# The taps of the short convolution in units 1 to 4 as 64x64 quarters of the array, on two token halves

## The chip, the cores and the metric

The kernel runs on one core of a Trainium2 chip. That core has a matrix engine (TensorE, PE in the profile, with its weight loads as PEld), a vector engine (VectorE, DVE), a scalar engine (ScalarE, ACT), GpSimd (POOL) and a queue engine (SyncE, SP) that issues almost every transfer of this kernel; the transfers themselves run on 16 DMA engines. The metric is the device time of one execution in microseconds (us). The median of three runs counts.

## The reference, cut to what matters

The reference is a block with two branches for 2048 tokens (S) and 640 channels (D). The part around the change is the first branch, a short causal convolution of `k` over four tokens, a product with `v`, and a long convolution over all tokens by a Fourier transform:

```python
for t in range(ks):                       # ks = 4 taps, one weight per channel and tap
    k_shift = k_shift + k_pad[:, t:t + S, :] * shift_k[:, ks - 1 - t][None, None, :]
kv = k_shift * v
...
kv_f = rfft(kv_pad); kf_f = rfft(ssm_k_pad)     # per channel, over 2*S tokens
y = irfft(kv_f * kf_f)[:S] + kv * ssm_D
x = x + ga * (h * y)                            # h: layer norm of x, modulated
```

The second branch is a gated MLP with a 2048x2048 mix over tokens. It uses all channels of the new `x` and so starts when the first branch is through. All inputs are bf16.

## The kernel before, in words

**Units.** The first branch is cut by channels into five units of 128 (0 to 4). For each unit `load_kv` brings `k` and `v` from device memory into a tile of the kind `big` with a transposing transfer, so that channels lie on the 128 partitions and tokens in a row (L520). Two such tiles exist, so unit 2 takes the place of unit 0. Unit 0 loads `k` and `v` in two halves of 1024 tokens each, the others in one transfer of 2048 tokens each.

**Taps.** `short_conv` makes four diagonal 128x128 matrices `dg` from the unit's tap weights (L531 to L539) and lets TensorE multiply `k`, shifted by 0 to 3 tokens, by them, so that four matmuls add up to one chunk of 512 tokens in PSUM (tile `sm`, L543 to L547). VectorE multiplies the chunk by `v` (L549 to L552). A unit has four chunks. The result is written to a scratch tensor in device memory, `kv_scr` (L558), and read back from there as `X<-kv_scr` in the layout of the Fourier transform (L389). After that a unit has two stages of matmuls forward (`s<-F1bd,X`, then `pu<-X,M`), a product with the transformed filter, and the same backward (`pz`). The filter itself comes in as `X<-in_A_ssm_k_dram` and goes through the same forward stages.

**The order.** Every step is recorded as an operation with its readers and writers, and a table of numbers, `ORDER`, says in which order all operations are issued. Each engine takes its own operations strictly in that order. On SP this means one queue for all loads and stores: the tapped products' store, the read-back, the filter's loads, the rows of `x` (`xt<-in_A_q_dram`), the modulation weights (`wm`) and the `k` and `v` of later units stand one behind the other. PE has one queue as well: the taps of a unit stand between transform matmuls of earlier units, so a tap that waits for its `k` holds back everything behind it. The names that matter below: `big` (k and v of a unit), `dg` (tap matrices), `sm` (PSUM of the taps), `X` (input of the transform), `kv_scr` (scratch), `ZT<-Z` (a transposing transfer inside the core for the end of a unit), `bsp` (a column of biases of the second branch, loaded later on by L1065).

Of the kernel before, what the change touches and what calls it, by code (L numbers as in the profile page):

```python
# [40 lines left out]
S2 G101 D18 S524 A1 D0 D100 G5 P7 A4 A10 D102 S82 G103 D121 D122 D104 D115 A531 S19 D13 D14 S20 D6 S21 A16 P1033 D532  # L41
A105 A106 S523 D15 A23 P1032 P8 P1035 S83 D11 P26 P24 S22 A533 D17 D116 D86 P1034 G107 G109 P145 A124 A146 P148 G108
D25 D110 A118 A117 A111 A112 A123 G36 D27 A149 A147 S88 D127 P28 D150 D113 P30 D87 D31 P154 A114 D527 D125 G119 P151
A155 A156 D29 A152 G126 D153 P133 D528 A128 A534 D134 G48 P139 D120 P159 P161 A160 D90 A140 S32 P136 P157 P142 A162
D529 P227 D137 P171 S34 A158 D530 A143 P163 D535 P39 A228 S33 A172 S35 P41 S84 G536 D138 A164 P167 S85 A168 P233 S46
P173 D42 A175 D40 S47 P176 A174 D177 A178 P43 D537 D44 P179 G553 P182 P37 D181 D549 D38 P165 G72 A180 A184 S45 A183
D141 G135 S526 P185 D186 A234 P229 G187 A166 P195 P211 G188 P49 P189 D196 P169 A230 D212 P231 A170 D50 P201 S3 D202
P217 P53 D218 A232 G144 A190 G550 P203 A542 P191 S89 S525 G197 G551 A204 P9 A12 P205 G198 G213 D54 P55 A543 P251 D192
P51 P247 D56 G130 G131 A252 G214 D206 P253 D52 A248 P239 A254 S565 A240 D538 P221 P199 D222 P257 G554 P241 P566 S91
A544 A200 D258 P568 P255 D539 P249 D256 P215 G223 D216 A242 G60 A545 A250 P193 G555 D93 P291 G224 S57 D292 S570 P225  # L50
S58 A540 P237 A238 P301 G207 P269 A194 P235 S59 P219 A569 A567 P571 D541 A302 G208 D270 A236 G271 P573 D546 A226 D220
D574 P307 P209 P245 G547 A552 P259 D572 D272 P67 D260 A308 P305 A246 P243 D548 D591 D561 D129 P265 A210 D68 G562 D261
A306 A244 A557 P61 P285 D62 A563 G262 P303 P65 P263 S92 P63 A304 D286 P325 A564 D266 S94 A326 D66 P295 P273 D296 P275
P327 A264 D276 S575 G707 A274 D676 S70 P267 D64 D297 P321 A328 A322 G556 G558 D651 D649 P309 A310 G670 P329 D96 P315
A330 S71 P576 P313 P331 P293 D559 D298 D577 A316 D597 S69 G287 P323 A314 D560 D595 S599 A332 P333 D598 D653 A324 G612
D593 P77 G288 P375 P349 A268 P277 D334 A294 A376 D78 D350 G594 S95 P343 P377 A132 D344 G596 P578 P319 G709 A378 P299
A278 P317 P73 D592 P379 D614 A320 A318 G335 A300 P311 P365 P289 D579 A380 G336 S97 G345 D616 A312 G652 P381 P337 D74
D654 P600 D674 D346 P279 D366 D601 D280 A290 G615 P369 P602 D370 P79 P347 G281 A382 A338 G282 D603 D80 A348 P387 P399
G371 A388 P359 P604 G372 G710 D605 P353 P283 G618 A400 D360 P401 P606 A284 D354 G355 D99 P351 P339 D340 A402 P403 D711
D607 A404 P383 D613 D619 P75 P385 A384 P405 P373 S580 A386 P395 D352 G361 G356 A406 G650 S620 A396 P397 P449 D362 A374  # L60
A398 P407 D76 P367 P413 A450 G617 P363 S81 D408 A368 D414 P391 P453 D364 P621 D622 P389 A392 A454 P439 P357 G655 G677
A390 P623 P451 A452 P427 D440 A358 D624 P341 G409 D428 P625 P417 G410 G611 G429 P455 D626 P411 P627 G430 S98 P443 P581
A342 A456 D418 P471 A412 P473 D444 P431 A472 A474 P393 P423 D628 G419 D656 A394 A582 G420 P475 P441 P465 A476 P479 D424
D432 G672 D442 P433 S657 A466 P421 A480 P461 G609 G629 D434 P477 A422 D639 P425 P658 G445 P467 A462 G446 A478 D671 P517
D659 A468 P447 A426 G435 P660 G436 D518 P457 A458 P437 A448 D661 P481 P463 G608 D482 P662 D663 G675 D631 G519 G520 G483
G484 A438 A464 P415 S583 P507 A416 P664 P497 D508 P584 D498 P485 P459 A486 P521 G634 S678 A460 A522 P491 G509 P1037
P501 D510 D633 A585 D492 P511 P487 D502 A512 G708 P499 A500 G493 G494 G503 P469 S586 G673 P495 D488 G504 S756 D665 P513
A470 P489 D514 P679 A496 G667 D680 P515 G712 D630 G666 A490 D632 P681 P505 A516 D682 P683 D637 D684 A506 P715 P719 A720
D716 P685 D686 P721 D687 A722 P717 P587 P723 D718 P725 D688 P726 P724 D689 D727 D728 D729 D730 D758 D759 D731 G669 P735
G692 D736 A588 P742 G760 D732 D761 G762 P1036 A763 G713 D690 P749 D734 P764 D743 D733 D691 D771 D766 S757 P765 D772  # L70
# [12 lines left out]
D1001 P1018 A949 P985 D998 D1062 G960 A947 D1002 D899 D1008 P989 A1019 A986 P956 D961 P1024 P1012 A964 D963 D962 D1009  # L83
A990 D987 A965 D991 P1014 D995 D984 A957 D988 A1025 A1013 G1026 A1015 D1051 P944 D1066 P1070 D1027 A945 D1063 A1030
P1020 A1029 S1042 D1064 P1072 A1071 D1028 A1021 D1031 D1065 P1074 D1068 D1067 P1077 D1075 P1081 P1022 A1073 P1076 D1069
D1078 D1082 D1079 P1083 S1080 P1010 P1016 A1017 D1084 A1011 S1085 D1047 A1023 D1061 D1046 D1048 D1060
"""


# [1215 lines left out]
```

## Time and profile before

| | |
|---|---|
| median of 3 runs | 312.03 us (311.89 to 312.06) |
| span of the profiled execution, first to last instruction | 309.7 us |
| outside the span (median less span) | 2.3 us |
| PE busy | 295.1 us (95%) in 2485 matmuls |
| DVE, POOL, ACT busy | 272.4, 186.2, 164.1 us |
| DMA, mean over the span | 146 GB/s, 45.23 MB in 127954 packets |

The profiled execution's own time is its span and the 2.3 us around it, taken from the median, since the profile gives only the span. The page has the busy time of each engine, the span in 40 slices, the chain of work that ended last, and the costliest groups of instructions. A group names the line, the engine, the operation and `out<-in` by the program's names. A line of a helper (L244 is the helper that issues a matmul) stands for all its callers, so such groups are told apart by their tiles. `SPq` is the issue of a transfer by SP; the time of such a row is the time the issue took, not the transfer's. How long a transfer takes to land stands in the list of DMA issues.

### The profile page before, as it was taken

To read this page: it belongs to the slowest core of one execution; us is meant where nothing else is said; L and a number is where in the kernel's file an instruction comes from. 1 tells how busy PE (TensorE), PEld (TensorE's weight loads), DVE (VectorE), ACT (ScalarE), POOL (GpSimd) and SP (SyncE) were. 2 spreads that over 40 slices of the span, in tenths; PEclk is the share of its full clock that TensorE was granted. 3 is DMA by queue.
4 is the path that set the end of the run, shared out by engine and by line. 5 is a ranking of instruction groups with operands and counts; after the bars stand their busy time and mean duration, and the time that the engine had idled before them with its cause. 6 is when DMAs were issued, how large, how long until landed. Compare 5 with 4: busy or idle time off the path is not lost.

```text
span 309.7 us, 6534 instructions
## 1 busy us (share of the span) xinstructions
PE 295.1 (95%) x2485; PEld 195.4 (63%) x2485; DVE 272.4 (88%) x532; ACT 164.1 (53%) x298; POOL 186.2 (60%) x209
## 2 busy tenths in 40 slices
PE   6979999999999999899999999998899999999995
PEld 1357678797889998755554555555455656565554
DVE  7797999999999999998859788999999878888574
ACT  4799699989787864466647799031111111021110
POOL 5724955856869999695705312049658474573922
PEclk9799999999999999999999999999999999999999
DMA  7999999999674949505898800073387593730323
GB/s 176 224 251 200 243 299 199 249 254 207 170 158 115 184 110 273 211 3 108 191 181 180 150 1 1 2 145 51 73 167 150 132 194 73 168 80 21 83 55 110
DMA packets 127954, 45.23 MB, mean 146 GB/s; under 512 B 117071, under 2 KB 127156, under 8 KB 127924
## 3 DMA queue, kind: packets, MB, share of 16 engines
q1 hardware_dynamic: 127770, 44.78, 65.5%
q8 instruction: 19, 0.31, 0.4%
q14 instruction: 11, 0.09, 0.1%
q10 hardware_dynamic: 154, 0.05, 0.1%
HBM read 16.11 MB, written 5.24 MB: 69 GB/s over the span
## 4 chain that ended last, share of the span: by engine, by line
PE 40%; DVE 6%; DMA 4%; SPq 4%; POOL 2%; issue 1%; ACT 0%; DVEq 0%; ACTq 0%
PE ps L1012 20%; PE po L1178 7%; PE pu L244 4%; PE pz L244 4%; DMA Z<-Z 3%; SPq L973 2%; PE pz L1012 2%; PE pu L1012 1%; DVE S L987 1%; PE po L1139 1%; SPq L1073 1%; DMA uT<-u 1%; POOL Z L844 1%; DVE V L1160 1%; POOL xt L697 1%
## 5 line engine op out<-in xcount | busy, mean ns | idle before, releaser
L244 PEld LDWEIGHTS <-Z 128*128 128x128 bf16 x320 | 31.1, 98 | 28.4 <-issue 1.2
L244 PE MATMUL pu<-X,M 128*128 128x128 bf16 (+1 forms) x480 | 45.9, 237 | 0.4 <-DVE Tf L461 0.3
L244 PEld LDWEIGHTS <-M 128*128 128x128 bf16 x480 | 37.1, 98 | 5.3 <-issue 0.6
L475 POOL TENSOR_TENSOR W<-Tf 128x256 bf16<-128x256 f32 x43 | 31.3, 745 | 12.7 <-DVE Tf L461 5.0
L1012 PEld LDWEIGHTS <-S 128*128 128x128 bf16 x256 | 25.0, 98 | 21.2
L244 PE MATMUL pu<-big,Z 128*128 128x432 bf16 x160 | 33.6, 346 | 0.5 <-ACT M L919 0.4
L244 PE MATMUL pz<-big,Z 128*128 128x432 bf16 x160 | 32.6, 346 | 0.1
L1196 ACT COPY O<-po 128x320 f32<-128x320 f32 x7 | 3.0, 427 | 55.9 <-PE po L1178 55.9
L247 ACT CAST X<-s 128x1024 bf16<-128x1024 f32 x30 | 30.7, 1024 | 3.5 <-PE s L244 3.4
L461 DVE TENSOR_TENSOR Tf<-pu,KH 128x1024 f32<-128x1024 f32 x25 | 30.0, 1214 | 1.4 <-PE pu L244 1.0
L1012 PEld LDWEIGHTS <-wT 128*128 128x128 bf16 x192 | 18.7, 98 | 17.6 <-issue 2.0
L244 PEld LDWEIGHTS <-G 128*128 128x128 bf16 x330 | 25.0, 98 | 3.3 <-issue 0.6
L247 ACT CAST KH<-pu 128x512 bf16<-128x512 f32 x40 | 23.5, 598 | 6.0 <-PE pu L244 6.0
L247 ACT CAST Z<-pz 128x512 bf16<-128x512 f32 x34 | 19.9, 599 | 8.2 <-PE pz L244 8.1
L1199 POOL TENSOR_TENSOR O<-O,xt 128x320 f32<-128x320 f32 x7 | 6.3, 906 | 28.0 <-ACT O L1198 28.0
L1012 PE MATMUL ps<-T,S 128*128 128x432 bf16 x112 | 22.7, 346 | 0.0
L1012 PE MATMUL ps<-X,wT 128*128 128x432 bf16 x112 | 22.7, 346 | 0.0
L244 PE MATMUL sm<-big,dg 128*128 128x512 bf16 (+1 forms) x80 | 21.3, 395 | 0.7 <-ACT dg L535 0.7
L1012 PE MATMUL ps<-X,S 128*128 128x432 bf16 x112 | 21.6, 346 | 0.0
L244 PEld LDWEIGHTS <-X 128*128 128x128 bf16 x288 | 18.2, 97 | 5.2 <-issue 1.4
L244 PE MATMUL s<-F1bd,X 128*128 128x256 bf16 x128 | 19.2, 273 | 0.3 <-ACT X L247 0.3
L925 DVE BATCH_NORM_STATS2 stz<-X 128x6 f32<-128x432 bf16 x32 | 17.8, 589 | 1.6 <-ACT X L919 1.6
(208 smaller groups left out, 679.9 us busy)
## 6 DMA issues: line engine op xcount, KB each, us to landing
wm<-in_w_mod_dram SPq DMA_DIRECT2D x6, 800.0 KB, 6.1
xt<-in_A_q_dram SPq DMA_DIRECT2D x4, 640.0 KB, 5.2
out_dram<-ot SPq DMA_DIRECT2D x15, 160.0 KB, 2.2
big<-in_B_w_in_dram SPq DMA_DIRECT2D x2, 1080.0 KB, 10.7
X<-in_A_ssm_k_dram SPq DMA_DIRECT2D x4, 512.0 KB, 7.0
kv_scr<-big SPq DMA_DIRECT2D x4, 512.0 KB, 3.2
X<-kv_scr SPq DMA_DIRECT2D x4, 512.0 KB, 4.5
w_o<-in_B_w_out_dram SPq DMA_DIRECT2D x6, 160.0 KB, 3.4
```

What stands on the lines that cost most here:

```text
L244: nc.tensor.matmul(o, lhsT=w, rhs=x, start=start, stop=stop)
L247: (e.copy if e is nc.scalar else e.tensor_copy)(dst, src)
L461: e.tensor_tensor(T_[:], (tl[pu] if src is None else tl[src])[:, :, :, None, :].to_broadcast(shape), tl[KH][:, :, None, :, :].to_broadcast ...
L475: e.tensor_tensor(tl[W][:, :, o, :], T_[:, :, 0, o, :], T_[:, :, 1, 1 - o, :], op=ALU.add if o else ALU.subtract)
L697: op("GD" if u < NU - 1 else "D", "res", lambda e: e.tensor_tensor(sl, sl, gl, op=ALU.add), r=[("gh", (u, g))], w=[("xt", (u, n)) for n in ...
L844: e.tensor_scalar(dst, xt[:, n, :], rstd2[:, n:n + 1], nmr2[:, n:n + 1], op0=ALU.mult, op1=ALU.add)
L925: op("D", "stz", lambda e, i=i, n=n, fc=fc: e.bn_stats(out=stz[:, n, fc, :], in_=tl[z2][:, i, fc * FC:(fc + 1) * FC]), r=[(z2, (i, fc))], ...
L973: nc.sync.dma_start_transpose(wTs[t][:], B_w_sp[t * P:(t + 1) * P, :])
L987: nc.vector.tensor_tensor(S[k][:], x, y, op=o)
L1012: nc.tensor.matmul(ps[:, :FC], lhsT=lhs[:, s_, :], rhs=rhs(s_), start=(s_ == 0 and not more), stop=(s_ == HT - 1), skip_group_check=more)
L1178: nc.tensor.matmul(ps[:, :HS], lhsT=w(k), rhs=x(k), start=start and k == 0, stop=stop and k == n - 1, skip_group_check=True)
L1199: nc.gpsimd.tensor_tensor(m5, m5, x_of(1, 1), op=ALU.add)
```

## The change

**Loads.** For units 1 to 4 the transposing load of `k` for all 2048 tokens becomes three loads. The first 1024 tokens come as before, with 128 channels. The last 1024 tokens and 32 tokens ahead of them (a halo, since taps reach back three tokens) come as two loads of 64 channels each, with the two halves of the channels exchanged: channels 64 to 127 land on partitions 0 to 63 and channels 0 to 63 on partitions 64 to 127. `v` moves up by the 32 columns of the halo.

**Taps.** For these units a diagonal 128x128 matrix is replaced by its two 64x64 diagonal blocks, in the order of channels and in the exchanged order. One operation now covers two chunks of 512 tokens, one of each token half, in two PSUM tiles, with 16 matmuls of 64x64 by 512: for each of four taps, four quarters of the array (rows 0 to 63 or 64 to 127, columns 0 to 63 or 64 to 127). The second half's output lands in the channels' right places. A unit has two such operations instead of four with four matmuls each.

**Small things.** The tap weights are turned into columns a second time in exchanged order (8 more small matmuls and a copy of twice the size at the start), and one more VectorE operation makes `ident2`, the two 64x64 identities. `ORDER` is written anew for the new numbers of operations.

```diff
 ORDER = """
-S2 G101 D18 S524 A1 D0 D100 G5 P7 A4 A10 D102 S82 G103 D121 D122 D104 D115 A531 S19 D13 D14 S20 D6 S21 A16 P1033 D532
+S3 G94 D19 S517 A2 D0 D1 D93 G6 P8 A5 A11 D95 S75 G96 D114 D115 D97 D108 A524 S20 D14 D15 S21 D7 S22 A17 P1026 D525 A98
...
-        sk = consta.tile([P, ND, 4], F32)
+        sk = consta.tile([P, 2, ND, 4], F32)
+        ident2 = consta.tile([P, P // 2], BF16)
...
-        SCH = 512
+        SCH, SH, HALO = 512, S // 2, 32
+        VO = S + HALO
...
-                    new(name, "big", [P, 2 * S])
-                src, o, m = (A_v if v else A_k), v * S, S // n
-                e.dma_start_transpose(tl[name][:, o + h * m:o + (h + 1) * m], src[0, h * m:(h + 1) * m, dt * P:(dt + 1) * P])
+                    new(name, "big", [P, VO + S])
+                src, o, m, cs = (A_v if v else A_k), VO if v else 0, S // n, slice(dt * P, (dt + 1) * P)
+                if v or dt == 0:
+                    e.dma_start_transpose(tl[name][:, o + h * m:o + (h + 1) * m], src[0, h * m:(h + 1) * m, cs])
+                    return
+                e.dma_start_transpose(tl[name][:, 0:SH], src[0, 0:SH, cs])
+                for r in range(2):
+                    e.dma_start_transpose(tl[name][r * QH:(r + 1) * QH, SH:VO], src[0, SH - HALO:, dt * P + (1 - r) * QH:dt * P + (2 - r) * QH])
...
+            quads = dt > 0
...
+            if quads:
+                for i in range(2):
+                    pss = ["tp%d_%d" % (dt, i + 2 * h) for h in range(2)]
+
+                    def quarters(e, i=i, pss=pss):
+                        p_ = [new(ps, "sm", [P, SCH], F32) for ps in pss]
+                        for j in range(4):
+                            lo = 0 if i else j
+                            for h, r in ((0, 0), (0, 1), (1, 0), (1, 1)):
+                                c_, l = r if h == 0 else 1 - r, lo if h == 0 else 0
+                                at = i * SCH - j + (SH + HALO if h else 0)
+                                nc.tensor.matmul(p_[h][c_ * QH:(c_ + 1) * QH, l:], lhsT=tl[dg][r * QH:(r + 1) * QH, h, j, :],
+                                                 rhs=tl[name][r * QH:(r + 1) * QH, at + l:at + SCH], start=j == 0, stop=j == 3,
+                                                 skip_group_check=True)
+                    op("P", "taps", quarters, r=[dg] + [(name, ("k", x)) for x in range(4)], w=pss, new=[(ps, "sm") for ps in pss])
+                    for h in range(2):
+                        op("D", "tv", lambda e, i=i + 2 * h, ps=pss[h]: times_v(e, i, ps), r=[pss[h]], w=[(name, ("v", i + 2 * h))])
...
+        op("D", "ident2", lambda e: e.tensor_tensor(ident2[:], ident[:, 0:QH], ident[:, QH:], op=ALU.add), r=["ident"], w=["ident2"])
```

How the instructions stand on two engines, before and in the change. The rows of SP around the loads of units 1 and 2 (`kv_scr<-big` is unit 0's store in two halves, `X<-kv_scr` its read-back) stood so before:

```order
L558 DMA kv_scr<-big 128x1024
L520 DMA_TRANSPOSE big<-in_A_k_dram 128x2048
L558 DMA kv_scr<-big 128x1024
L520 DMA_TRANSPOSE big<-in_A_v_dram 128x2048
L389 DMA X<-kv_scr 128x8x128 x2
L520 DMA_TRANSPOSE big<-in_A_k_dram 128x2048
L520 DMA_TRANSPOSE big<-in_A_v_dram 128x2048
```

and stand so in the change:

```order
L591 DMA kv_scr<-big 128x1024
L525 DMA_TRANSPOSE big<-in_A_k_dram 128x1024
L527 DMA big<-in_A_k_dram 64x1056x1 x2
L591 DMA kv_scr<-big 128x1024
L523 DMA_TRANSPOSE big<-in_A_v_dram 128x2048
L390 DMA X<-kv_scr 128x8x128 x2
L525 DMA_TRANSPOSE big<-in_A_k_dram 128x1024
L527 DMA big<-in_A_k_dram 64x1056x1 x2
L523 DMA_TRANSPOSE big<-in_A_v_dram 128x2048
```

The transposing load of 2048 tokens has become one of 1024 tokens, and behind it stand two transfers of 64 channels by 1056 tokens. These two are not of the kind `DMA_TRANSPOSE`; they are plain transfers whose innermost run is one element, `64x1056x1`. The store of unit 0's second half and its read-back stand behind those of unit 1.

The rows of SP around the last such load, unit 4's (`kv_scr<-big` is unit 3's store, `ZT<-Z` belongs to unit 0's end, the last `X<-kv_scr` is unit 3's read-back), stood so before:

```order
L619 DMA wm<-in_w_mod_dram 128x5x640
L520 DMA_TRANSPOSE big<-in_A_k_dram 128x2048
L520 DMA_TRANSPOSE big<-in_A_v_dram 128x2048
L558 DMA kv_scr<-big 128x2048
L684 DMA_TRANSPOSE ZT<-Z 128x32x128
L389 DMA X<-kv_scr 128x16x128
```

and in the change:

```order
L652 DMA wm<-in_w_mod_dram 128x5x640
L525 DMA_TRANSPOSE big<-in_A_k_dram 128x1024
L527 DMA big<-in_A_k_dram 64x1056x1 x2
L523 DMA_TRANSPOSE big<-in_A_v_dram 128x2048
L591 DMA kv_scr<-big 128x2048
L717 DMA_TRANSPOSE ZT<-Z 128x32x128
L390 DMA X<-kv_scr 128x16x128
```

Nothing changes places here, and again two plain transfers have come in.

The rows of PE at the first taps of unit 4 (`pu<-X,M` ahead of them and `s<-F1bd,X` behind them belong to the transforms of other units) stood so before:

```order
L244 MATMUL pu<-X_1063,M_80 128x128
L244 LDWEIGHTS dg
L244 MATMUL sm<-big,dg 128x512
L244 LDWEIGHTS dg
L244 MATMUL sm<-big,dg 128x512
```

and in the change:

```order
L245 MATMUL pu<-X_1108,M_80 128x128
L571 LDWEIGHTS dg
L571 MATMUL sm<-big,dg 64x512
L571 LDWEIGHTS dg
L571 MATMUL sm<-big,dg 64x512
L571 LDWEIGHTS dg
L571 MATMUL sm<-big,dg 64x512
```

Four weight loads and matmuls of 128 columns have become sixteen of 64 columns (the rows repeat). They stand at the same place of the queue, in front of the same matmuls.

More of the change, by code (lines that the diff above doesn't have):

```diff
@@ L539, in short_conv @@
-            op("DGA", "diag", diag, r=["sk", "ident"], w=[dg], new=[(dg, "dg")])
-            for i in range(S // SCH):
-                ps = "tp%d_%d" % (dt, i)
-                def taps(e, i=i, ps=ps):
-                    p_ = new(ps, "sm", [P, SCH], F32)
-                    for j in range(4):
-                        lo = 0 if i else j
-                        mm(p_[:, lo:], tl[dg][:, j, :], tl[name][:, i * SCH - j + lo:(i + 1) * SCH - j], j == 0, j == 3)
-                def times_v(e, i=i, ps=ps):
-                    o = S + i * SCH
-                    vsl = tl[name][:, o:o + SCH]
-                    e.tensor_tensor(vsl, tl[ps][:], vsl, op=ALU.mult)
-                op("P", "taps", taps, r=[dg, (name, ("k", i))] + ([(name, ("k", i - 1))] if i else []), w=[ps], new=[(ps, "sm")])
-                op("D", "tv", times_v, r=[ps], w=[(name, ("v", i))])
+                new(dg, "dg", [P, 2, 4, QH] if quads else [P, 4, P])
@@ new lines, in diag @@
+                if quads:
+                    eye, w_, shape = ident2[:, None, None, :], sk[:, :, dt, :, None], [P, 2, 4, QH]
+                else:
+                    eye, w_, shape = ident[:, None, :], sk[:, 0, dt, :, None], [P, 4, P]
+                if e is nc.scalar:
+                    for j in range(8 if quads else 4):
+                        if quads:
+                            e.mul(tl[dg][:, j // 4, j % 4, :], ident2[:], sk[:, j // 4, dt, j % 4:j % 4 + 1])
+                        else:
+                            e.mul(tl[dg][:, j, :], ident[:], sk[:, 0, dt, j:j + 1])
+                    return
@@ new lines, in diag, with times_v, taps @@
+                e.tensor_tensor(tl[dg][:], eye.to_broadcast(shape), w_.to_broadcast(shape), op=ALU.mult)
+            op("DGA", "diag", diag, r=["sk", "ident2" if quads else "ident"], w=[dg], new=[(dg, "dg")])
+            def times_v(e, i, ps):
+                o = VO + i * SCH
+                vsl = tl[name][:, o:o + SCH]
+                e.tensor_tensor(vsl, tl[ps][:], vsl, op=ALU.mult)
+            if quads:
+                for i in range(2):
[13 more added lines that the diff above has]
+                        op("D", "tv", lambda e, i=i + 2 * h, ps=pss[h]: times_v(e, i, ps), r=[pss[h]], w=[(name, ("v", i + 2 * h))])
+            else:
+                for i in range(S // SCH):
+                    ps = "tp%d_%d" % (dt, i)
+                    def taps(e, i=i, ps=ps):
+                        p_ = new(ps, "sm", [P, SCH], F32)
+                        for j in range(4):
+                            lo = 0 if i else j
+                            mm(p_[:, lo:], tl[dg][:, j, :], tl[name][:, i * SCH - j + lo:(i + 1) * SCH - j], j == 0, j == 3)
+                    op("P", "taps", taps, r=[dg, (name, ("k", i))] + ([(name, ("k", i - 1))] if i else []), w=[ps], new=[(ps, "sm")])
+                    op("D", "tv", lambda e, i=i, ps=ps: times_v(e, i, ps), r=[ps], w=[(name, ("v", i))])
```

104 lines of the change are left out of this document (51 added, 53 removed).

## The prediction

> **What bounds the kernel now.** I read the page first: its span, the busy shares and the chain that ended last.
>
> ```profile
> span 309.7 us, 6534 instructions
> PE 295.1 (95%) x2485; PEld 195.4 (63%) x2485; DVE 272.4 (88%) x532; ACT 164.1 (53%) x298; POOL 186.2 (60%) x209
> PE 40%; DVE 6%; DMA 4%; SPq 4%; POOL 2%; issue 1%; ACT 0%; DVEq 0%; ACTq 0%
> ```
>
> PE is busy for 95% of the span and leads the chain. So cheaper taps should be worth their time on PE. But the change also touches loads. So I read the busy time by stage next, in stretches of 15 us up to 90 us (the columns are busy time and number of instructions of each engine, the granted clock, the DMA engines' busy share and GB/s).
>
> ```profile
> 0.00:15.00 15.00, 11.19 (x40) 4.33 (x41) 10.70 (x40) 8.86 (x23) 9.98 (x20) 0.89 0.90 199
> 15.00:30.00 15.00, 13.04 (x121) 9.33 (x120) 13.06 (x39) 14.20 (x28) 5.16 (x6) 1.00 1.10 225
> 30.00:45.00 15.00, 14.36 (x141) 10.94 (x140) 14.04 (x18) 12.14 (x24) 10.76 (x14) 1.00 0.98 262
> 45.00:60.00 15.00, 15.00 (x155) 12.06 (x153) 14.79 (x31) 14.58 (x30) 9.78 (x12) 1.00 1.05 227
> 60.00:75.00 15.00, 15.00 (x164) 12.65 (x163) 14.89 (x25) 13.93 (x21) 9.27 (x10) 1.00 1.10 242
> ```
>
> From 30 us on PE hardly pauses, and up to 75 us the DMA engines are busy all the time too (a share above 1 means that packets overlap). A transfer added to this stage finds no gap to hide in; it pushes everything behind it on SP's queue. That is why I look at the loads before the matmuls. Unit 4's taps are the last that wait for `k`; these are its load on SP, the read-back of unit 3 some rows behind it, and its first taps on PE with the group behind them:
>
> ```profile
> 58.83 4.71 SPq L520 DMA_TRANSPOSE big<-in_A_k_dram  x1
> 73.20 0.53 SPq L389 DMA_DIRECT2D X<-kv_scr  x1
> 70.02 1.03 PE L244 MATMUL sm<-big,dg 128*128 128x512 bf16 x4
> 70.88 0.60 PE L244 MATMUL s<-F1bd,X 128*128 128x256 bf16 x4
> ```
>
> **The change, part by part.** *The taps on PE.* Four full matmuls start 0.22 us apart (70.02 to 70.88 us, where the next group starts, for four). The change removes 64 of them, 14.1 us, and adds 128 quarters of the same 512 columns. If four quarters share the array, these take 32 times 0.22 us, 7.0 us, and PE gains 7 us; if they follow one another, they take 28 us and PE loses 14 us. No row shows which. A quarter of that falls to each unit, and it counts for unit 4 alone, since before the others PE will wait anyway (below): 1.8 us less to 3.5 us more. I put in nothing and keep both ends.
>
> *The loads of k.* Here the order of the change says what the diff doesn't: the two loads of 64 channels are plain transfers with runs of one element, `64x1056x1`. Each has 64 times 1056, 67,584 elements of 2 bytes. The trace of before has one transfer of this kind, the bias column `bsp`, with 2048 elements of 2 bytes in 4 KB. This is its row among the DMA issues (the last number is us from issue to landing), beside that of the transposing loads of `k` and the shortest of the list; and behind them the packet counts of five stretches of its time, the whole (152.2 to 154.7 us) and then 153.1 to 153.2, 154.0 to 154.5, 154.4 to 154.5 and 154.55 to 154.65 us:
>
> ```profile
> bsp<-in_B_b_sp_dram SPq DMA_DIRECT2D x1, 4.0 KB, 6.0
> big<-in_A_k_dram SPq DMA_TRANSPOSE x6, 6.2
> KH<-in_A_ssm_D_dram SPq DMA_DIRECT2D x1, 1.2 KB, 1.6
> DMA packets 2281, 0.24 MB, mean 96 GB/s; under 512 B 2097, under 2 KB 2281, under 8 KB 2281
> DMA packets 178, 0.01 MB, mean 144 GB/s; under 512 B 167, under 2 KB 178, under 8 KB 178
> DMA packets 366, 0.00 MB, mean 1 GB/s; under 512 B 366, under 2 KB 366, under 8 KB 366
> DMA packets 44, 0.00 MB, mean 1 GB/s; under 512 B 44, under 2 KB 44, under 8 KB 44
> DMA packets 17, 0.00 MB, mean 0 GB/s; under 512 B 17, under 2 KB 17, under 8 KB 17
> ```
>
> Between 154.0 and 154.5 us there are 366 packets at 1 GB/s: some 2 bytes each. So such a transfer is one packet per element, and its price goes by packets, not bytes. Three rates can be read from these rows, and they bound the price of one load.
> - The last stretch has 17 packets in 0.1 us. I read it as one DMA engine finishing alone, a packet every 5.9 ns; 44 in the stretch before it are then two to three engines, and 167 at the peak are ten. With 16 engines, each has 67,584/16 = 4224 packets: 24.8 us a load.
> - The peak itself, 167 in 0.1 us: 40.5 us a load.
> - All 2048 in 2.5 us: 82.5 us a load. In part of that time other transfers were still on the engines.
>
> I take a value near the first: the others count engines that had not begun or were already done. To 24.8 us I add 3.3 us. One engine's share of `bsp` needs 128 times 5.9 ns, 0.75 us, while the whole spread over 2.5 us, so the engines stood 1.7 us apart; and the shortest landing of the list is 1.6 us. That makes 28.1 us, an estimate, and for eight loads 225 us. Both ends, 24.8 and 82.5 us, go into the rivals. The Trainium skill (DMA: Bandwidth & Descriptors, Rules for kernel authors) says that a plain transfer with a rearranged pattern is 19 times as slow as the transposing one; from the 6.2 us for 262,144 elements that would be an estimate of 30.4 us a load and 18 us more in the sum. No run here shows that ratio yet.
>
> *What is saved.* The transposing loads of `k` lose their second 1024 tokens, at these issue times (the first row is two loads of 1024):
>
> ```profile
> 2.20 4.40 SPq L520 DMA_TRANSPOSE big<-in_A_k_dram  x2
> 22.74 4.22 SPq L520 DMA_TRANSPOSE big<-in_A_k_dram  x1
> 46.98 4.24 SPq L520 DMA_TRANSPOSE big<-in_A_k_dram  x1
> ```
>
> Some 2.1 us for each of four units, 8.4 us.
>
> *Who waits.* PE stops at the first taps of units 1, 2, 3 and 4 until that unit's two loads are through. Behind them on PE stand the transforms of the earlier units, so DVE, ACT and POOL run dry as well. On SP's queue the store of unit 0's second half and its read-back stand behind unit 1's loads, and each later read-back behind the next unit's. Between units 2 and 3 SP has a second wait of its own: unit 2's store needs its taps, and behind it stand unit 3's loads.
>
> ```profile
> 33.38 1.02 PE L244 MATMUL sm<-big,dg 128*128 128x512 bf16 x4
> 43.19 1.56 SPq L558 DMA_DIRECT2D kv_scr<-big  x1
> xt<-in_A_q_dram SPq DMA_DIRECT2D x4, 640.0 KB, 5.2
> wm<-in_w_mod_dram SPq DMA_DIRECT2D x6, 800.0 KB, 6.1
> ```
>
> From unit 2's first taps (33.38 us) to unit 3's load (46.98 us) are 13.6 us. In it move v, a read-back and a filter's load (512 KB each), rows of `x` (640 KB) and `wm` (800 KB), 2976 KB, at the 262 GB/s of that stretch 11.4 us. So some 2 us go by with the DMA engines idle. The four waits themselves need no other price: they are the DMA time, counted once.
>
> *The small things.* The tap weights' eight more matmuls and the copy sit ahead of the first taps, and `ident2` is one small VectorE operation. Before, PE waits there for the first tap matrix:
>
> ```profile
> 9.13 0.39 PE L244 MATMUL sm<-big,dg 128*128 128x512 bf16 x1 [0.70 <-ACT dg L535]
> 2.20 0.29 PE L244 MATMUL sm<-ident,KH 5*128 5x5 bf16 x4 [2.20 <-DMA KH<-in_A_shift_k_dram]
> ```
>
> Four such matmuls take 0.29 us, so eight delay the matrix by 0.6 us. I cost that at nothing: it is hidden by the wait for unit 1's loads. Without that cover it would cost the 0.6 us. The tap matrices have the same 512 columns as before, and the products with `v` the same number.
>
> *The sum.* Unit 4's `k` landed at 58.8 + 6.2 = 65.0 us. Less 8.4, plus 225, plus 2: it lands at 283.6 us, and there the taps that stood at 70.02 us begin. All that lies behind them takes as long as before, 309.7 - 70.0 = 239.7 us, as PE had no gaps there that a later start would fill. What could be late next is unit 3's read-back, which follows unit 4's loads: it was issued at 73.20 us, 8.2 us after unit 4's `k` landed, and PE needed it at 82.54 us, 12.5 us after its taps:
>
> ```profile
> 82.54 0.60 PE L244 MATMUL s<-F1bd,X 128*128 128x256 bf16 x4
> X<-kv_scr SPq DMA_DIRECT2D x4, 512.0 KB, 4.5
> ```
>
> With its 4.5 us to landing that is 12.7 us: just in time, nothing added. The span becomes 523.3 us. The profiled execution has 309.7 us of span, the median of the runs is 312.0, so 2.3 us lie outside; with them the forecast is **525.6 us**, some 68% more than before.
>
> **The rivals.**
> - *The loads of one element run at the peak or below it, because more engines at once do not all keep 5.9 ns.* For it: ten engines are the most that a stretch shows. Against it: 17, 44 and 167 packets fit one rate for one to ten engines. At 40.5 us a load the sum is 525.6 + 8 x 12.4 = 625 us.
> - *Something ahead of the engines makes the packets, at the mean rate.* For it: the whole transfer kept to 82.5 us a load. Against it: the peak is twice that. The time would be 525.6 + 8 x 54.4 = 961 us.
> - *The loads cost by bytes, and the change does what its words say.* Two loads of half the channels then take what the removed half took, 2.1 us, and hide as before; PE is the bound and gains up to 7 us: 312.0 - 7 = 305 us, faster. This turns on whether 67,584 packets are made at all. For it: the bytes are the same. Against it: the 366 packets of 2 bytes.
> - *The loads run fast and the quarters one after another.* PE loses 14 us, all on its path: 326 us. Against it stands the same row.
>
> **How the numbers follow.** The forecast, loads at 24.8 to 34 us, has a chance of 0.57 and its own range of 490 to 575 us. The peak rate has 0.22, the mean rate 0.12, the loads by bytes 0.04, fast loads with slow quarters 0.02; 0.03 are left for anything else. The low end of the range is the sum with 24.8 us a load, 499 us, less the 1.8 us of the quarters, the 2 us of idling and some us for engines that start closer together, 490 us. The high end takes in the peak rate (625 us), the quarters' 3.5 us and 2.7 us more on each of the eight loads, 22 us: 650 us. The mean rate lies outside, as do the fast loads. About 0.2% is what runs of this kernel can tell from no change. Faster by more than that are the loads by bytes, 0.04; within it 0.01; slower all the others, 0.95.
>
> **What would show it.** Right: four long gaps of PE, each ended by the landing of `big<-in_A_k_dram`; in section 2 of the page DMA busy there while GB/s falls to a few; some 540,000 more packets under 512 B; a plain `big<-in_A_k_dram` row among the issues with tens of us to landing; PE busy changed by less than 15 us. The length of the gaps gives the price of a load. Wrong: as many packets as before, or gaps that end on something else. If the gaps are there but at 80 us a load, the step that failed is the reading of one engine's rate from the last stretch.

## The result: 1015.9 us, 3.25 times the time before

The changed kernel takes 1015.87 us (median of 4 runs, 1009.68 to 1018.76) against 311.96 us for the kernel before on the same chip (4 runs, 311.40 to 312.06). The ratio is 3.2522, with a 95% interval of 3.2428 to 3.2616. The forecast of 525.6 us had the direction and the place right, and the size wrong; the time lies outside the range.

The page of the changed kernel, its span, busy shares, slices (each 25.4 us long) and packets:

```profile
span 1016.9 us, 6689 instructions
PE 310.5 (31%) x2556; PEld 201.1 (20%) x2557; DVE 272.9 (27%) x533; ACT 165.1 (16%) x298; POOL 186.9 (18%) x209
PE   7000000110000008100000320000008899998997
DMA  9999999999999999999999999999995666524743
GB/s 157 1 1 2 2 2 2 63 2 2 2 2 2 2 14 218 2 2 2 2 2 2 105 3 2 2 1 2 2 32 127 158 163 140 107 61 93 143 92 69
DMA packets 664659, 45.28 MB, mean 45 GB/s; under 512 B 653775, under 2 KB 663860, under 8 KB 664628
```

PE has the same work as before (310.5 us against 295.1), but it stands still in four long stretches, in which the DMA engines are fully busy at 1 or 2 GB/s. There are 536,705 more packets, all of them small, and as many bytes as before. So the loads of one element are what the prediction took them for. Their price is not. The list of DMA issues on the page (KB each, us from issue to landing) and the waits of PE (us in all, times, longest) show it:

```profile
big<-in_A_k_dram SPq DMA_DIRECT2D x8, 132.0 KB, 137.3
```

```profile
PE sm L571 <- DMA big<-in_A_k_dram: 675.2, 8, 91.2
```

So do the timelines of SP and of PE at these loads (start, time; on SP the time of the issue):

```profile
16.86 92.55 SPq L527 DMA_DIRECT2D big<-in_A_k_dram  x2
201.55 88.38 SPq L527 DMA_DIRECT2D big<-in_A_k_dram  x2
398.99 88.16 SPq L527 DMA_DIRECT2D big<-in_A_k_dram  x2
581.43 91.10 SPq L527 DMA_DIRECT2D big<-in_A_k_dram  x2
761.06 1.86 PE L571 MATMUL sm<-big,dg 64*64 64x512 bf16 x13 [82.21 <-DMA big<-in_A_k_dram]
```

PE waits eight times, once for each load, 675.2 us in all, 84.4 us a load, and the two issues of a unit hold SP's queue for some 90 us. The packets of 2 bytes run in four blocks (19.0 to 195.2, 203.2 to 378.1, 402.3 to 572.9 and 584.7 to 758.0 us), 695 us for eight loads: 86.9 us each, where the prediction had put 28.1. Unit 4's first taps are through their last wait at 761.06 us. Before, they started at 70.02.

### The profile page after: what moved, and what is told of

It reads as the page before. It is cut to its first block, busy times and chain, and to the rows that moved or that the text cites. A ratio compares the mean times of both kernels' runs of the same rounds, so it can differ in the third digit from the quotient of the medians.

```text
span 1016.9 us, 6689 instructions
## 1 busy us (share of the span) xinstructions
PE 310.5 (31%) x2556; PEld 201.1 (20%) x2557; DVE 272.9 (27%) x533; ACT 165.1 (16%) x298; POOL 186.9 (18%) x209
## 5 line engine op out<-in xcount | busy, mean ns | idle before, releaser
L571 PE MATMUL sm<-big,dg 64*64 64x512 bf16 (+3 forms) x128 | 17.3, 514 | 678.9 <-DMA big<-in_A_k_dram 675.2
L559 DVE TENSOR_TENSOR big<-sm,big 128x512 bf16<-128x512 f32 x20 | 13.5, 684 | 687.7 <-DMA big<-in_A_v_dram 344.2
L571 PEld LDWEIGHTS <-dg 64*64 64x64 bf16 x128 | 5.3, 126 | 686.1 <-issue 507.6
L248 ACT CAST X<-s 128x1024 bf16<-128x1024 f32 x30 | 30.8, 1026 | 344.8 <-PE s L245 344.7
L245 PE MATMUL pu<-X,M 128*128 128x128 bf16 (+1 forms) x480 | 49.9, 249 | 3.9 <-DVE Tf L462 2.1
L245 PEld LDWEIGHTS <-M 128*128 128x128 bf16 x480 | 39.4, 103 | 12.0 <-issue 6.5
L640 POOL TENSOR_SCALAR gh<-xt,rstd,nmr 128x640 bf16<-128x640 bf16 x8 | 7.7, 959 | 178.2 <-DVE nmr L632 177.1
L245 PE MATMUL s<-F1bd,X 128*128 128x256 bf16 x128 | 21.9, 300 | 2.5 <-ACT X L248 1.5
L248 ACT CAST Z<-pz 128x512 bf16<-128x512 f32 x34 | 19.9, 599 | 7.4 <-PE pz L245 7.1
```

Of the source, the lines that this page charges most:

```text
L245: nc.tensor.matmul(o, lhsT=w, rhs=x, start=start, stop=stop)
L248: (e.copy if e is nc.scalar else e.tensor_copy)(dst, src)
L559: e.tensor_tensor(vsl, tl[ps][:], vsl, op=ALU.mult)
L571: nc.tensor.matmul(p_[h][c_ * QH:(c_ + 1) * QH, l:], lhsT=tl[dg][r * QH:(r + 1) * QH, h, j, :], rhs=tl[name][r * QH:(r + 1) * QH, at + l:a ...
L640: e.tensor_scalar(gh[:, n, :], xt[:, n, :], rstd1[:, n:n + 1], nmr1[:, n:n + 1], op0=ALU.mult, op1=ALU.add)
```

## The experiments

### The loads alone

The kernel before, with its order and its full taps, in which only the second 1024 tokens of `k` in units 1 to 4 come as two plain loads of 64 channels, in their own places:

```diff
-                e.dma_start_transpose(tl[name][:, o + h * m:o + (h + 1) * m], src[0, h * m:(h + 1) * m, dt * P:(dt + 1) * P])
+                if v or dt == 0:
+                    e.dma_start_transpose(tl[name][:, o + h * m:o + (h + 1) * m], src[0, h * m:(h + 1) * m, dt * P:(dt + 1) * P])
+                    return
+                e.dma_start_transpose(tl[name][:, 0:S // 2], src[0, 0:S // 2, dt * P:(dt + 1) * P])
+                for r in range(2):
+                    e.dma_start_transpose(tl[name][r * QH:(r + 1) * QH, S // 2:S], src[0, S // 2:, dt * P + r * QH:dt * P + (r + 1) * QH])
```

> The kernel before with full taps, and only its loads changed: the second 1024 tokens of k in units 1 to 4 as two plain loads of 64 channels, not exchanged. Theory A: 8 loads of 65,536 elements at the 86.9 us per 67,584 that the changed kernel shows, 84.3 us each, so 1016 - 8 x 2.6 = 995 us, give or take 12. Theory B: part of the 704 us belongs to the quarters or to the new order; then it stays below 950 us.

Measured: 973.15 us (2 runs), ratio 3.1178 (3.1088 to 3.1268). So the loads alone bring 661 of the change's 704 us. PE's wait in this run:

```profile
PE sm L244 <- DMA big<-in_A_k_dram: 648.6, 4, 168.8
```

The time is 22 us under the 995 us that I expected, 10 us below the low end, and above the 950 us of theory B, so neither theory has it. The shorter loads, without a halo, were in my 995 us already. Two terms are smaller than I had them. The four blocks of 2-byte packets, each from its first to its last, take 663.8 us in this run, 83.0 us a load instead of 84.3, which makes 10 us. And from the end of unit 4's wait (727.61 us) it takes 242.3 us, 13.5 us less than the 255.8 us of the change (1016.9 - 761.1). So not quite all of the 704 us are the loads': some 15 us come with the change's other parts.

### All but the loads

The changed kernel, in which the second half of `k` comes in one transposing load of 128 channels:

```diff
-                for r in range(2):
-                    e.dma_start_transpose(tl[name][r * QH:(r + 1) * QH, SH:VO], src[0, SH - HALO:, dt * P + (1 - r) * QH:dt * P + (2 - r) * QH])
+                e.dma_start_transpose(tl[name][:, SH:VO], src[0, SH - HALO:, cs])
```

> The change with its quarters, but the second half of k comes in one transposing load of 128 channels and 1056 tokens, without the exchange of the channel halves (so the second half's channels come out exchanged, and the values computed from them differ; the work is the same). Theory A, the two plain loads are the whole loss: the time falls from 1016 us to that of before or below it; in the changed kernel 13 to 16 quarters take 1.86 us at a granted clock of 0.50, so four run side by side and PE gains up to 7 us: 305 to 312 us. Theory B, the quarters cost time of their own (one after another, or by draining the array): above 315 us, 326 us if they run one after another.

Measured: 330.65 us (6 runs, 329.26 to 332.75) against 312.16, ratio 1.0594 (1.0554 to 1.0634). The 700 us are gone, but 18.5 us of loss remain. So there is a second, smaller cause that has nothing to do with small packets. My theory A said 305 to 312 us and is wrong; the time lies where theory B put it, but not for its reason, as the next runs show. The rows below are a stretch in which PE falls far behind, a window of 15 us (columns as in the prediction), first of the kernel before, then of this one:

```profile
90.00:105.00 15.00, 15.00 (x230) 14.10 (x227) 14.73 (x18) 12.23 (x20) 14.57 (x16) 1.00 0.70 136
```

```profile
90.00:105.00 15.00, 12.35 (x154) 10.52 (x154) 10.48 (x17) 8.49 (x12) 8.79 (x11) 0.89 0.00 1
```

All engines have slack, and the DMA engines do nothing. SP's queue is stuck. Its timeline, and PE's at the products `sm<-Ebd,ZT`, which read the transposed tile `ZT`; first before:

```profile
67.25 5.86 SPq L684 DMA_TRANSPOSE ZT<-Z  x1
85.57 4.79 SPq L684 DMA_TRANSPOSE ZT<-Z  x1
85.11 0.40 PE L244 MATMUL sm<-Ebd,ZT 128*128 128x64 bf16 x8
```

and in this kernel:

```profile
73.69 5.75 SPq L716 DMA_TRANSPOSE ZT<-Z  x1
104.50 4.73 SPq L716 DMA_TRANSPOSE ZT<-Z  x1
104.02 0.39 PE L245 MATMUL sm<-Ebd,ZT 128*128 128x64 bf16 x8 [0.55 <-DVE gh L709]
```

There is one `ZT` buffer. In both kernels the second transposing transfer starts within 0.1 us of the end of the last product on the first `ZT`. In the new order that product comes 30.3 us after the first transfer instead of 17.9. Until then SP can issue nothing behind it: unit 4's store, its read-back, the next loads. The changed kernel itself has the same: its two `ZT<-Z` stand at 759.60 and 789.63 us, 30.0 us apart.

### The quarters, the order and the pairs apart

Three more kernels, all with the transposing load just shown. In the first the quarters become full 128x128 matmuls, in pairs and in the change's order:

```diff
-                        for j in range(4):
-                            lo = 0 if i else j
-                            for h, r in ((0, 0), (0, 1), (1, 0), (1, 1)):
-                                c_, l = r if h == 0 else 1 - r, lo if h == 0 else 0
...
+                        for h in range(2):
+                            for j in range(4):
+                                l = 0 if i or h else j
...
+                                mm(p_[h][:, l:], tl[dg][:, j, :], tl[name][:, at + l:at + SCH], j == 0, j == 3)
```

> As the run with whole loads of k (330.7 us), in the change's own order and with its two operations a unit that fill two PSUM tiles each, but with the eight full 128x128 matmuls of the two chunks instead of sixteen quarters. Theory O, the new order and the pairing cost the 18 us over the kernel before: 330 to 336 us, the quarters' gain on PE being lost as well. Theory C, the quarters themselves cost them (a switch of the array's form, or a clock that falls): 312 to 318 us.

In the second the quarters stay, and the table of the order is that of the kernel before, with the two pairs of a unit at or near the places where its first and third chunk stood. On SP the two orders are the same. On PE they differ at the pairs and at the `y` products of unit 0 (`sm<-Ebd,ZT`), which read `ZT`, and on VectorE at what reads these. This is a piece of the table, PE's numbers alone; 68 and 71 are unit 4's pairs, 593 to 599 the `y` products:

```diff
-P374 P330 P272 P362 P340 P68 P593 P380 P392 P352 P346 P276 P394 P344 P332 P396 P376 P378 P398 P366 P388 P390 P442 P400 P595 P597 P599
+P374 P330 P593 P272 P362 P595 P340 P71 P380 P392 P352 P597 P346 P276 P394 P599 P344 P332 P396 P376 P378 P398 P366 P388 P390 P442 P400
```

> The whole loads and the quarters of the change, but the order of the kernel before for everything else: each pair of chunks stands where the second or third of the four chunks of its unit stood, and unit 0's end and the rows behind it stand where they stood. Theory O: 305 to 314 us. Theory C: 320 us or more, since the same 128 quarters run.

The third has this order and the full matmuls of the first, so that of the change's larger parts only the pairs are left:

> The same order, with eight full matmuls instead of sixteen quarters in each pair. It shows what the quarters alone are worth: if four run side by side and PE is the bound, 4 to 7 us more than with the quarters; if PE waits for others at these places, within 1 us of it. Theory O: 310 to 318 us. Theory C: below 314 us and below the run with quarters.

| kernel (transposing loads) | us | ratio to before |
|---|---|---|
| quarters, new order | 330.65 | 1.0594 (1.0554 to 1.0634) |
| full matmuls, new order | 330.76 | 1.0607 (1.0582 to 1.0631) |
| quarters, old order | 319.18 | 1.0225 (1.0191 to 1.0259) |
| full matmuls, old order | 317.46 | 1.0187 (1.0160 to 1.0213) |

Rows 1 and 3 give the cost of the order with quarters, 11.5 us, rows 2 and 4 with full matmuls, 13.3 us. I had expected 305 to 314 us for row 3 and missed it; row 4 lies within its 310 to 318 us. Rows 1 and 2, and rows 3 and 4, show that the quarters bring nothing in either order. In the last row 5.8 us are left against its kernel before (311.64 us).

The order costs in two places. One is the wait for `ZT`: with the `y` products back in their old place the two transfers stand 24.1 us apart instead of 30.8 with quarters, and 20.6 instead of 27.9 with full matmuls, while SP's queue stands the same. The other lies ahead of it. The second pairs of units 1 to 3 stand later on PE in the new order, behind 135, 230 and 444 other matmuls instead of 127, 216 and 400, and the stores wait for them: unit 3's goes out at 73.30 us instead of 67.23 (quarters). Unit 4's first taps stand behind the same 505 matmuls in all four kernels; so their start shows what is lost by then. These are the rows in the new order, with quarters and with full matmuls:

```profile
78.54 1.06 PE L570 MATMUL sm<-big,dg 64*64 64x512 bf16 x16
78.28 1.89 PE L245 MATMUL sm<-big,dg 128*128 128x512 bf16 x8
```

In the old order they start at 70.53 and 73.51 us (rows below). So 8.0 us of the order's cost with quarters, and 4.8 us with full matmuls, are lost before the first `ZT<-Z` holds anything up. No run moves the pairs and the `y` products one at a time, so how the rest divides is not shown.

Why do the quarters bring nothing? They are faster on PE. Its timeline in the old order: the taps of two chunks and the group behind them, unit 4's first taps, and a group behind its last ones. First with quarters, then with full matmuls:

```profile
27.80 1.06 PE L571 MATMUL sm<-big,dg 64*64 64x512 bf16 x16
28.79 0.39 PE L246 MATMUL pz<-F1bd,X 128*128 128x256 bf16 x2
...
70.53 1.06 PE L571 MATMUL sm<-big,dg 64*64 64x512 bf16 x16
...
90.80 0.38 PE L246 MATMUL s<-F1bd,X 128*128 128x256 bf16 x2
```

```profile
27.90 1.89 PE L246 MATMUL sm<-big,dg 128*128 128x512 bf16 x8
29.63 0.38 PE L246 MATMUL pz<-F1bd,X 128*128 128x256 bf16 x2
...
73.51 1.89 PE L246 MATMUL sm<-big,dg 128*128 128x512 bf16 x8
...
90.70 0.49 PE L246 MATMUL s<-F1bd,X 128*128 128x256 bf16 x3
```

Sixteen quarters hold PE for 0.99 us, eight full matmuls for 1.73. Four quarters share the array; over eight pairs that saves 5.9 us. By unit 4's first taps the kernel with quarters is 3.0 us ahead (70.53 against 73.51 us). At the group near 90.7 us they are level. Between the two PE waits for VectorE. These are PE's rows there with quarters, and then with full matmuls:

```profile
82.27 0.61 PE L246 MATMUL pu<-X,M 128*128 128x256 bf16 x6 [1.63 <-DVE T L463]
85.72 1.05 PE L571 MATMUL sm<-big,dg 64*64 64x512 bf16 x14 [1.83 <-DVE gh L710]
```

```profile
84.88 1.03 PE L246 MATMUL sm<-big,dg 128*128 128x512 bf16 x4
87.40 1.02 PE L246 MATMUL sm<-big,dg 128*128 128x512 bf16 x4 [1.49 <-DVE gh L705]
```

PE waits 2.3 us longer for VectorE there than with full matmuls (three waits, 3.81 us, against one, 1.49). VectorE is busy for 10.67 of the 10.70 us from 75.0 to 85.7 us: it sets the pace, and the quarters take nothing from it. Then the clock takes its part: the window from 75 to 90 us ran at a granted clock of 0.90 instead of 1.00, and the same groups, from behind unit 4's second pair to the row near 90.7 us, took 4.09 us instead of 2.44. Such a dip isn't in every run with quarters. Of the six, the one whose mean granted clock was 1.000 took 317.5 us, the one at 0.984 took 320.6. So even at the full clock the quarters do no better than the full matmuls (317.46 us).

The last two rows show a cost of the pairs as well: a pair needs two `sm` buffers at once, and there are two in all, which the products `sm<-Ebd,ZT` use too. The second half of the pair stands until VectorE's `gh` operation has emptied one. Before, a chunk's four matmuls needed one buffer. That makes a wait of 1.49 us with full matmuls; a third buffer wasn't tried. It is not the whole of the 5.8 us. By unit 1's first taps nothing is lost against the kernel before (23.95 against 24.10 us), so the small things at the start cost nothing, as forecast. By unit 4's first taps 3.5 us are (73.51 against 70.02), ahead of this wait. What makes these 3.5 us is not shown.

The split of the load could have been part of it. So it was run alone, in the kernel before:

```diff
-                e.dma_start_transpose(tl[name][:, o + h * m:o + (h + 1) * m], src[0, h * m:(h + 1) * m, dt * P:(dt + 1) * P])
+                if v or dt == 0:
+                    e.dma_start_transpose(tl[name][:, o + h * m:o + (h + 1) * m], src[0, h * m:(h + 1) * m, dt * P:(dt + 1) * P])
+                    return
+                for r in range(2):
+                    e.dma_start_transpose(tl[name][:, r * (S // 2):(r + 1) * (S // 2)], src[0, r * (S // 2):(r + 1) * (S // 2), dt * P:(dt + 1) * P])
```

> The kernel before, with its order and its full taps, in which the one transposing load of 2048 tokens of `k` is issued as two of 1024 tokens, in units 1 to 4. It separates two readings of the 5.5 us (1.9%) that the paired taps with full matmuls in the old place lose. Reading A: the second transfer and its issue on SP's queue cost them, since the queue's work behind it moves; then this kernel loses 3 us or more (ratio 1.010 or above). Reading B: the pairs cost them, because two `sm` buffers must be free at once and eight matmuls stand in one piece; then this kernel stays within 1 us of the kernel before (ratio 0.997 to 1.003). I hold B with 0.75.

Measured: 311.79 us (10 runs), ratio 0.9991 (0.9972 to 1.0011). The split costs nothing. So the 5.8 us belong to what is left of the change in that kernel: the pairs, and with them the 32 tokens of halo in each second load, which no run takes out alone.

### The price of an element load

Isolated loads ahead of the kernel before, one after the other, each to a tile of its own and waited for by a small VectorE copy. `TK` is 1056, so the first is the load of the change; the `q` are 2, 4, 8 and 16 rows of 2048 elements; `pi` and `pj` are issued at once by two engines. The lines that make each load wait for the one before (`after`) are left out here:

```diff
+        nc.sync.dma_start_transpose(pa[:], ks_[0:TK, 64:128])
+        nc.sync.dma_start_transpose(pb[:, 0:TK // 2], ks_[0:TK // 2, 64:128])
+        nc.sync.dma_start(q2[:], turned(slice(0, 2048), slice(64, 66)))
...
+        nc.sync.dma_start(pg[:, :, 0], A_v[0].rearrange("s c -> (s c)")[0:64 * TK].rearrange("(p t) -> p t", p=64))
+        nc.sync.dma_start(pc[:], ph[:, :, 0])
+        nc.sync.dma_start_transpose(pi[:], ks_[0:TK, 64:128])
+        nc.scalar.dma_start_transpose(pj[:], ks_[0:TK, 0:64])
+        nc.sync.dma_start(pd[:], A_v[0].rearrange("s c -> (s c)")[0:64 * TK].rearrange("(p t) -> p t", p=64))
+        nc.sync.dma_start(pe_[:].rearrange("p (s two) -> p s two", two=2), ks_[0:TK // 2, 0:P].rearrange("s (p two) -> p s two", two=2))
```

> Eleven loads ahead of the kernel before, each alone on the queue (the next is issued when the one before has landed). All but the last two move single elements of 2 bytes: 64 rows of 1056 as in the change (a), half of its tokens (b), 2, 4, 8 and 16 rows of 2048, which occupy 2, 4, 8 and 16 DMA engines (q2 to q16), 64 x 1056 from consecutive addresses (g), the same from on-chip memory to on-chip memory (c), two loads like a at once from two issuing engines (i, j); then 64 rows in whole (d), and 33,792 runs of 4 bytes (e). Theory S, one maker of packets for all engines, 1.25 ns a packet: a 86 us, b 43, q2 12 (an engine alone 5.9 ns), q4 12, q8 20, q16 41, g 86, c 86, e 42; i and j together 172. Theory N, every engine slows to 20 ns a packet when the load is long: q2, q4, q8 and q16 all 41 us. Theory M, the memory's rows 1280 bytes apart are slow: a 86, but g and c near 25 us. Theory Q, a maker for each issuing queue: i and j together 86 us. By bytes: a no longer than d, 2 to 4 us.

VectorE's timeline in this run, without the rows of 4 and 8 (72.94 and 70.38 us). The number in brackets is its wait, from issue to landing:

```profile
89.01 0.14 DVE L197 COPY tok<-pa 2x1 bf16<-2x1 bf16 x1 [86.88 <-DMA pa<-in_A_k_dram]
133.66 0.14 DVE L197 COPY tok<-pb 2x1 bf16<-2x1 bf16 x1 [44.33 <-DMA pb<-in_A_k_dram]
186.47 0.14 DVE L197 COPY tok<-q 2x1 bf16<-2x1 bf16 x1 [52.49 <-DMA q<-in_A_k_dram]
401.15 0.14 DVE L197 COPY tok<-q 2x1 bf16<-2x1 bf16 x1 [70.39 <-DMA q<-in_A_k_dram]
510.51 0.14 DVE L197 COPY tok<-pg 2x1 bf16<-2x1 bf16 x1 [109.04 <-DMA pg<-in_A_v_dram]
597.46 0.14 DVE L197 COPY tok<-pc 2x1 bf16<-2x1 bf16 x1 [86.62 <-DMA pc<-ph]
768.27 0.14 DVE L197 COPY tok<-pi 2x1 bf16<-2x1 bf16 x1 [170.43 <-DMA pi<-in_A_k_dram]
772.07 0.14 DVE L197 COPY tok<-pd 2x1 bf16<-2x1 bf16 x1 [2.77 <-DMA pd<-in_A_v_dram]
794.41 0.14 DVE L197 COPY tok<-pe 2x1 bf16<-2x1 bf16 x1 [22.01 <-DMA pe<-in_A_k_dram]
```

- The load of the change, alone on the chip's DMA engines, takes 86.88 us; half of it takes half. So nothing in the kernel's traffic made it slow.
- As many 2-byte elements from memory on the core (`pc<-ph`) take 86.62 us, so device memory isn't the limit. In rows of 2112 bytes the same bytes take 2.77 us.
- Two at once on two issuing engines take 170.43 us, twice one. So the two queues share what limits them.
- Two rows of 2048 elements go through two engines: while 2, 4, 8 and 16 rows are loaded, the busy share of the 16 engines is 0.24, 0.49, 0.98 and 1.97. The two rows take 52.49 us for 2048 packets on each: 24.5 ns a packet, less 2.3 us of landing (below). Sixteen rows on sixteen engines need 70.39 us for as many packets on each. Eight times the engines move eight times the packets at 0.75 of the speed. So the price is one of each engine and not of a common maker of packets ahead of them; by that theory, S, the two rows would have taken 12 us. My theory N had this shape, but not the size (41 us for each of these).
- 33,792 runs of 4 bytes take 22.01 us, half of what as many runs of 2 bytes need.

The packet records of this run at the first load, from 3.7 to 5.7 us, from 20 to 22 us, and from 85.9 us to its landing at 89.0:

```profile
DMA packets 3355, 0.01 MB, mean 3 GB/s; under 512 B 3355, under 2 KB 3355, under 8 KB 3355
DMA packets 1594, 0.00 MB, mean 2 GB/s; under 512 B 1594, under 2 KB 1594, under 8 KB 1594
DMA packets 0, 0.00 MB, mean 0 GB/s; under 512 B 0, under 2 KB 0, under 8 KB 0
```

The records start at twice the later rate, and they end 3.1 us ahead of the landing. Either the first packets are cheap, or their records run ahead of the work. A second run of the kind, with shorter loads, tells these apart:

```diff
+        for t_, n_, nxt in zip(small, (32, 64, 128, 256, 512), small[1:] + [w4]):
+            nc.sync.dma_start(t_[:], turned(slice(0, n_), slice(64, 128)))
+            after([t_], [nxt])
+        for t_, w_, nxt in ((w4, 4, [w8]), (w8, 8, [])):
+            nc.sync.dma_start(t_[:].rearrange("p (s w) -> p s w", w=w_), ks_[0:528, 0:64 * w_].rearrange("s (p w) -> p s w", w=w_))
+            after([t_], nxt)
```

> The kernel before, with seven isolated loads ahead of it, each waited for by VectorE before the next is issued; only these waits count, the whole time says nothing. Five loads of runs of 2 bytes to 64 rows of 32, 64, 128, 256 and 512 elements: 128, 256, 512, 1024 and 2048 packets for each of 16 engines. Then two loads of 33,792 runs each, of 8 and of 16 bytes. Theory A (each engine takes some 200 packets fast, at 6 to 8 ns, and every later one at 20 ns): 3.0 to 4.0 us for 128 packets, 4.5 to 6 for 256, then 20 ns more for every packet: 10, 20 and 41 us. Theory B (20 ns for every packet from the first, and some 2.7 us of landing): 5.3, 7.9, 13.0, 23.3 and 43.9 us. Under A the 2048 elements of `bsp`, 128 for each engine, lie wholly in the fast part, and no row of them could show the later price. For the runs of 8 and 16 bytes: if the price from 4 bytes up goes by packets alone, 22 us for both, as for 4 bytes; if it goes on halving with the length of the run, 11 and 6 us; if by bytes, 44 and 88 us.

VectorE's timeline of this run, with the five loads of 2-byte runs and the two of 8 and 16 bytes:

```profile
5.88 0.14 DVE L192 COPY tok<-l 2x1 bf16<-2x1 bf16 x1 [4.84 <-DMA l<-in_A_k_dram]
13.33 0.14 DVE L192 COPY tok<-l 2x1 bf16<-2x1 bf16 x1 [7.13 <-DMA l<-in_A_k_dram]
25.98 0.14 DVE L192 COPY tok<-l 2x1 bf16<-2x1 bf16 x1 [12.33 <-DMA l<-in_A_k_dram]
48.85 0.14 DVE L192 COPY tok<-l 2x1 bf16<-2x1 bf16 x1 [22.54 <-DMA l<-in_A_k_dram]
92.22 0.14 DVE L192 COPY tok<-l 2x1 bf16<-2x1 bf16 x1 [43.04 <-DMA l<-in_A_k_dram]
114.44 0.14 DVE L192 COPY tok<-w 2x1 bf16<-2x1 bf16 x1 [21.90 <-DMA w<-in_A_k_dram]
136.99 0.14 DVE L192 COPY tok<-w 2x1 bf16<-2x1 bf16 x1 [22.23 <-DMA w<-in_A_k_dram]
```

And its packet counts from 2.4 to 3.8 us, and from there to the landing of the first load:

```profile
DMA packets 2064, 0.00 MB, mean 3 GB/s; under 512 B 2064, under 2 KB 2064, under 8 KB 2064
DMA packets 0, 0.00 MB, mean 0 GB/s; under 512 B 0, under 2 KB 0, under 8 KB 0
```

My theory A, some 200 fast packets first, falls. From 128 to 2048 packets on an engine the landing takes 38.20 us more, 19.9 ns a packet, and from 128 to 256 already 17.9 ns. So a load takes 2.3 us and 20 ns for every packet on an engine; theory B had the price right and the 2.3 us as 2.7. That the first 128 packets are no cheaper was not measured by itself, but there is little room for it: the load of whole rows took 2.77 us in all, so of the 4.84 us at least 2.07 are left for 128 packets, an estimate of 16 ns each or more. The records give them less. All packets of this load are in the records between 2.4 and 3.8 us, 11 ns each, and then nothing is recorded for 2.1 us until it lands at 5.88. So the records run ahead of the work; what lets them is not shown. Runs of 8 and of 16 bytes take 22 us like those of 4: from 4 bytes up the price goes by packets alone, at 9.3 ns, and a packet of 2 bytes costs twice that.

None of these kernels is faster than the kernel before.

## Why the prediction was right and wrong

**The mechanism was right.** Four stretches of waiting, ended by the landing of `big<-in_A_k_dram`, DMA busy at a few GB/s, 536,705 more packets (540,000 forecast). PE's busy time grew by 15.4 us, where less than 15 was named; with transposing loads it is 296.1 us, so nearly all of the growth comes with the waits, behind which PE runs at a granted clock of 0.50 (last section).

**The step that failed is the price of one element load.** The prediction put it thus: "The last stretch has 17 packets in 0.1 us. I read it as one DMA engine finishing alone, a packet every 5.9 ns." The load takes 86.9 us, not 28.1. The 5.9 ns were a rate of records that run ahead of the transfer, and the reading by single engines has no ground either: 167 packets in 0.1 us, taken for ten engines, is also the mean rate in the first 2 us of the isolated load (3355 packets), which runs on all sixteen engines. `bsp` with its 128 packets on an engine is the size of the first load of the second run; both have all their records in within 1.4 to 2.5 us. The trace of before held the sign: the last of the records of `bsp` is at 154.70 us, but it landed only at 156.8, where VectorE had waited for it:

```profile
156.87 0.17 DVE L1080 CAST bcol<-bsp 128x16 f32<-128x16 bf16 x1 [2.42 <-DMA bsp<-in_B_b_sp_dram]
```

The row from which to price it was the landing, 6.0 us from issue. Less the 1.6 us of the shortest landing, that makes 34 ns a packet and 145 us a load: too much (a load of that size alone lands in 4.84 us, and a transposing load of `wT` ran beside this one), but above the truth, and as a bound it would have opened the range.

The rival at the mean rate named 82.5 us a load and 961 us, close to what came. That was luck: its reason fell, as each engine has the price for itself and no maker of packets ahead of them, and its 2.5 us were a spread of records that takes 1.4 us when such a load runs alone. The rival at the peak rate, 40.5 us a load, fell with the records.

**What the sum would have been.** With 86.9 in place of 28.1 the sum is 525.6 + 8 x 58.8 = 996 us. Two other terms were short. Outside the eight loads I had 58.6 us up to unit 4's `k` (65.0 - 8.4 + 2); it was 66 us (761.1 - 695), 7.5 us more. And behind unit 4's first taps I had 239.7 us as before; it was 255.8 (1016.9 - 761.1), 16 us more. With both it is 1019.5 us, where the profiled execution took 1018.8. This puts measured terms together and shows only that none is left out; it doesn't explain the last two.

**The tail as before was the second miss.** I had looked at the order around the loads only ("Nothing changes places here"), and taken the rest as unchanged. In the kernel with transposing loads the tail is 251.1 us (329.6 - 78.54), 11.4 us longer than before without a single slow load. The wait for `ZT` lies in it, but the old order shortens the tail only to 247.6 us with quarters, and from 250.1 to 241.7 us with full matmuls (the spans less the start of unit 4's first taps). So the order is one part of it and the pairs another, and how they share the 11.4 us is not settled; nor are the other 4.7 us of the 16. The rest of what the order costs with quarters, 8.0 us, falls ahead of unit 4's first taps, where the sum had nothing for it either; behind the slow loads it can't be told apart.

**The quarters were costed at nothing, and with transposing loads that is what they bring, for a reason that I did not have.** I had kept both ends, 1.8 us less and 3.5 more. The rows show that quarters share the array: 0.99 against 1.73 us a pair, 5.9 us in all where I had 7 for that case. The rival in which they run one after another fell. But VectorE, at 88% busy before, is the next to be waited for, and with a dip of the clock it took the gain back in the same stretch. No run has full matmuls behind the slow loads, so there their worth is not shown. The rival at 305 us would not have come even with cheap loads: 330.65 us came, and 319.18 with the old order.

The Trainium skill (DMA: Bandwidth & Descriptors, Rules for kernel authors) puts a plain rearranged transfer at 19 times the transposing one. Here it is more: scaled by elements, an estimate, 6.2 us for 262,144 elements are 1.6 us for 67,584, and 86.88 us are 54 times that. The same section says that issuing from several engines doesn't help, as they share the DMA engines; the 170.43 us for two at once agree.

## What to carry to other kernels

Price an unknown transfer by the time to its landing, never by the rate at which its packet records appear, and where the trace holds only a short one, keep the whole landing divided by the packets of one engine as the upper bound. Before a transposing load is cut, look in the order whether the pieces are still transposing transfers; a piece of 64 channels was not, and its 132 KB cost 87 us. When a table of the order is written anew, compare not only the rows around the change but every buffer that exists once: how far its next writer stands behind its last reader decides what a whole queue waits for. And look at the last piece of work that a store waits for: if that moves back, all that stands behind the store moves back with it.

## What the runs showed of the hardware that I had not expected

- Packet records ran 2.1 us (128 packets on an engine) to 3.1 us (4224) ahead of the landing, and over their first 2 us at twice the rate that lasts.
- A packet of 2 bytes cost 20 ns on its engine, one of 4, 8 or 16 bytes 9.3 ns. Writing the 2-byte elements 4 bytes apart did not help: 109.04 us, 25 ns a packet. Where an engine wrote one row only (sixteen rows on sixteen engines) a packet cost 33 ns, with two rows on two engines, also one row each, 24.5 ns. What makes these differences was not looked for.
- PE's granted clock was 0.52 to 0.54 in the stretches of waiting. Behind the second of them it was 0.50 from 380.9 to 384 us, 0.59 to 388 and 1.00 from there on. The rows of PE in the changed kernel, right behind a long wait and 11.6 us later:

```profile
380.96 1.86 PE L571 MATMUL sm<-big,dg 64*64 64x512 bf16 x13 [84.60 <-DMA big<-in_A_k_dram]
392.52 1.06 PE L571 MATMUL sm<-big,dg 64*64 64x512 bf16 x16
```

The first row has thirteen quarters, as three of the sixteen had run before the wait ended (two at 211.12 us, one at 295.78). Thirteen took 1.86 us behind the wait, sixteen 1.06 us later: a quarter took about twice as long. So a stage that starts after a long stall pays some twice for its first microseconds.
